# Last group's slots and four turns inside the attention's last two units, layers joined, half of the output weights split in the first expert

## The chip, the cores and the metric

The kernel runs on one core of one Trainium2 chip. Time is device microseconds of that core, from the first to the last instruction and what lies around them; the median of three runs is 391.73 us (389.76 to 392.42).

## The reference

Three layers follow one another: a retention-like attention, a soft mixture of eight experts over 32 slots, and a bilinear layer.

```python
def _attn_ref(q, k, v):                     # 8 x 8 heads, 576 positions, 64 wide
    scores = scale * np.matmul(q, k.transpose(0, 1, 3, 2))
    Dmat = np.where(rel >= 0, gamma[:, None, None] ** rel[None, :, :], 0.0)
    return np.matmul(scores * Dmat[None, :, :, :], v)

def _moe_ref(x, phi, w1, w2):               # x 4608 x 512, 8 experts of 4 slots, F = 1024
    logits = x @ phi
    d = softmax of logits over the tokens;  c = softmax of logits over the slots
    slot_input = (d.T @ x).reshape(E, S_per_e, D)
    for e in range(E):
        slot_out[e] = np.maximum(slot_input[e] @ w1[e], 0.0) @ w2[e]
    return c @ slot_out.reshape(n_slots, D)

def _moe2_ref(x, w1, w2, w3, w_out):
    return ((x @ w1) * (x @ w2) @ w3) @ w_out
```

## The kernel before, in words

All instructions are emitted in an order written out by hand (`manual_schedule`), so each engine runs its own list in program order, and SyncE (SP) issues nearly all transfers, each waiting in turn for its place.

**Attention.** 36 units `u` of 128 tokens (`NU` = 36; `T, r = divmod(u - 4, 4)` counts groups of four, which lag by four units). A unit does `emit_pv`, `emit_xt` (VectorE writes the unit's x into `xts[u % 6]`), `emit_state`, `emit_qk` of unit u + 2, `emit_turns` (L210: eight transposes of x of unit u - 4 into the PSUM tile `pair`, and one ScalarE copy to `xgs`), and `emit_inter`. Every fourth unit does the running softmax of a group: `emit_logits`, `emit_exp`, `emit_dT` (transpose of the weights, copied by ScalarE to `dt`), `emit_z` and `emit_slots` (eight matmuls into a slot sum, which VectorE adds to `acc`). Behind the loop the tail (L835 to L902) does what is left for the last two groups: `emit_logits(8)`, `emit_slots(7)`, four transposed x (`emit_xtr`), the column maxima, `emit_slots(8)` and the scaling that gives `slotm`, the input of the experts.

**Pieces.** The weights `wo`, `m1`, `m2` and `w3` come as 64-bit words in 40 pieces of 512 KB. `conv_list` (L489) turns a piece into float32 by two ScalarE and three VectorE operations, and `add` (L520) ends it on GpSimd. Pieces of `m1`, `m2` stay in `mw_sb`; pieces of `wo` (j < 8) and `w3` pass through three slots of `vals` and are split into a high and a low part, by a ScalarE cast (`copy`, L528) and a GpSimd subtraction (`sub`, L533). `emit_Ws` (L552) emits steps of the product w3 x wo, three matmuls each, 64 in all; step 4 i + k reads piece i of w3 and quarter 4 (i % 2) + k of `wo`.

**Experts.** Weights come in 64 loads of 512 KB (`load_expert`, L578), eight to an expert, each into a place from the list `free`; 21 places of 4 KB a partition are used for the attention's buffers first and come free near its end. For expert e, `emit_l1` (32 matmuls), ScalarE's relu to `hr`, VectorE's transpose to `ht` (`emit_turned`, at tick 1), and `emit_l2` (16 matmuls) at tick 2 of four. In each tick steps of `emit_Ws` are emitted up to a target written in L956, and `soft` emits the softmax over the slots, whose odd steps put two transposes on TensorE. After the experts come `a`, `b` and their products (L993 to L1105) and nine output groups (L1117).

Of the kernel before, what the change touches and what calls it, by code (L numbers as in the profile page):

```python
# [31 lines left out]
def retention_softmoe_bilinear(  # L32
# [51 lines left out]
    wop = const.tile([128, 8192], F32R, name="wop")  # L84
# [45 lines left out]
    ring = [place("ew0")]  # L130

# [76 lines left out]
    turned = pair.rearrange("p (a z k j) -> p z a k j", a=2, z=2, k=4)  # L208

# [251 lines left out]
    woh, wol = wop[:, 0:4096], wop[:, 4096:8192]  # L461
# [8 lines left out]
    nth = lambda j: j if j < 8 else j - 16  # L470

    def value(j):
        t = mw_sb[:, 512 * (j - 8):] if 8 <= j < N3 else vals[:, 512 * (nth(j) % 3):]
        return t[:, 0:512]
# [39 lines left out]
    def high_low(j):  # L514
        if j < 8:
            return woh[:, 512 * j:512 * j + 512], wol[:, 512 * j:512 * j + 512]
        t = block(w3p, (j - N3) % 3)
        return t[:, 0:512], t[:, 512:1024]

    def add(i):  # L520
# [3 lines left out]
        if not 8 <= j < N3:  # L524
            copies.append(j)
# [26 lines left out]
    def emit_Ws(n, lag=1):  # L552
        for _ in range(n):
            i, k = divmod(nW[0], 4)
            if i == 16 or nsplit[0] < min(9 + i + lag, 24):
                return
# [5 lines left out]
            bh, bl = (t[:, 512 * k8:512 * k8 + 512] for t in (woh, wol))  # L562
# [92 lines left out]
    with tc.manual_schedule():  # L655
# [72 lines left out]
        free.extend(ring)  # L728
        came, TWICE, PACED = [], (10, 14, 18, 22, 26), 3

        def can_conv():
# [3 lines left out]
            return 8 <= j < N3 or nth(j) < nsplit[0] + 3  # L735
# [14 lines left out]
        for u in range(NU):  # L750
# [51 lines left out]
            if u >= 2:  # L802
                ended = emit_turns(u - 4, u + 4)
# [16 lines left out]
            if u >= 7 and r == 3:  # L820
# [20 lines left out]
        free.extend([*p_places, s_place])  # L841
# [8 lines left out]
        emit_slots(T - 1, False)  # L850
        emit_exp(T)
        add_slots(T - 1)
        emit_z(T - 1)
        emit_z(T)
        mfin = st["m"]
        pr = bank[0]
        emit_xtr(NU - 4)
# [5 lines left out]
        emit_xtr(NU - 3, nc.vector.tensor_copy)  # L863
        emit_dT(T)
        emit_xtr(NU - 2)
        emit_xtr(NU - 1, nc.vector.tensor_copy)
        free.extend(xt_places)
# [54 lines left out]

        nsoft = [0]
# [14 lines left out]
        for e in range(NE):  # L938
# [11 lines left out]
            for t in range(4):  # L950
# [5 lines left out]
                emit_Ws(max(0, (min(5, 3 + step), min(7, 1 + step), min(55, 7 + (step - 8) * 48 // 20))[min(e, 2)] - nW[0]))  # L956
                if e == NE - 1 and t == 1:
                    emit_Ws(3, 0)
                if t == 2:
                    emit_l2(e)  # L960
                    if len(wplaces) < 8:
# [20 lines left out]
        left = [t for t in map(tag_of, qb + vb + rb + kb + p_places + [s_place, kt_place] + xt_places) if t not in [second, *map(tag_of, wplaces)]]  # L982
# [7 lines left out]
        ph, pl = (wop[:, 4096 * i:4096 * i + 4096].rearrange("p (c n) -> p c n", c=8) for i in range(2))  # L990
# [224 lines left out]
```

## Time and profile before

| what | us |
|---|---|
| median of three runs | 391.73 (389.76 to 392.42) |
| the profiled execution, whole | 393.84 |
| its span, first to last instruction | 392.1 |
| TensorE busy | 375.4 (96%) |
| VectorE, ScalarE, GpSimd busy | 257.4, 199.0, 172.6 |
| attention, to the last `emit_pv` | 0 to 161 |
| tail, to the first expert's layer 1 | 161 to 172.7 |
| experts, to the end of the last layer 2 | 172.7 to 246.3 |
| products | 246 to 281 |
| output groups | 281 to 392 |

The stages are read from the first matmul of their lines in the trace. A matmul's end in it is modelled, so busy TensorE time can hold waits; where an engine really stood is told by the wait in brackets behind a row.

### The profile page before, as it was taken

The numbers are of one execution on the slowest core, as the hardware profiler recorded it, in microseconds if no ns is written. First come the engines' busy times: TensorE is split into PE (matmuls) and PEld (weight loads), VectorE is DVE, ScalarE is ACT, GpSimd is POOL, SyncE is SP. The second block draws the span as 40 slices with busy tenths as digits, with TensorE's granted clock in tenths as the row PEclk, the third lists the DMA queues.
The fourth block names the chain that finished last, engine by engine and source line by source line (L and its number), as shares of the span: only waits on it lengthen the run. The fifth ranks groups of instructions, "written<-read, shape, count | busy, mean of one in ns | idle before, by whom it ended". The sixth has DMA issues, their size and how long they took to land.

```text
span 392.1 us, 10958 instructions
## 1 busy us (share of the span) xinstructions
PE 375.4 (96%) x4447; PEld 284.9 (73%) x4447; DVE 257.4 (66%) x432; ACT 199.0 (51%) x424; POOL 172.6 (44%) x158
## 2 busy tenths in 40 slices
PE   6999999999997999799999999999999999999996
PEld 3888787878876897564666664678688777788774
DVE  4648999899896889555477963399766445355500
ACT  2347696788675787423364532234445353544432
POOL 2733765675464436202345652127544334552420
PEclk9999999999999999999999999999999999999999
DMA  7999899899988999999999999692359989998634
GB/s 241 335 331 333 301 365 323 252 375 376 291 274 313 305 324 331 325 397 371 410 409 408 410 407 389 153 210 39 82 114 207 232 221 227 235 222 210 158 89 103
DMA packets 48211, 108.75 MB, mean 277 GB/s; under 512 B 7584, under 2 KB 10016, under 8 KB 48160
## 3 DMA queue, kind: packets, MB, share of 16 engines
q1 hardware_dynamic: 47008, 107.85, 86.4%
q8 instruction: 35, 0.57, 0.6%
q10 hardware_dynamic: 1152, 0.20, 0.3%
q14 instruction: 16, 0.13, 0.1%
HBM read 97.41 MB, written 10.62 MB: 275 GB/s over the span
## 4 chain that ended last, share of the span: by engine, by line
PE 74%; DVE 14%; DMA 8%; issue 2%; ACT 1%; POOL 1%; ACTq 0%; POOLq 0%; DVEq 0%
PE bank L564 10%; PE bank L1131 9%; PE bank L1133 8%; PE bank L1132 8%; PE output L282 6%; PE scores L253 5%; DMA kr<-in_v 4%; PE output L316 4%; PE bank L622 3%; PE bank L602 3%; PE state L296 3%; DMA v<-in_ew 2%; PE one L356 2%; PE bank L1122 2%; PE pair L215 2%; DVE vals L497 2%
## 5 line engine op out<-in xcount | busy, mean ns | idle before, releaser
L646 POOL TENSOR_TENSOR cc<-mw_sb,cc 128x512 fp32r<-128x512 f32 x36 | 46.0, 1297 | 56.5 <-ACT cc L645 56.5
L523 POOL TENSOR_TENSOR vals<-vals,msb 128x512 int32<-128x512 int32 x24 | 30.8, 1284 | 46.7 <-DVE vals L497 44.5
L564 PE MATMUL bank<-wop,w3p 128*128 128x512 f32 x192 | 50.0, 404 | 0.0
L263 DVE TENSOR_TENSOR pm<-scores,msb 128x1024 f32<-128x1024 f32 x31 | 37.8, 1220 | 15.0 <-PE scores L253 14.8
L564 PEld LDWEIGHTS bank<-wop,w3p 128*128 128x128 f32 x192 | 34.4, 188 | 14.4 <-issue 7.1
L645 ACT CAST cc<-mw_sb 128x512 fp32r<-128x512 f32 x36 | 22.2, 616 | 43.6 <-DVE mw_sb L644 34.8
L1131 PE MATMUL bank<-w3p,cc 128*128 128x512 f32 x108 | 43.1, 399 | 0.0
L1133 PE MATMUL bank<-w3p,cc 128*128 128x512 f32 x108 | 42.1, 390 | 0.0
L1132 PE MATMUL bank<-w3p,cc 128*128 128x512 f32 x108 | 42.0, 389 | 0.0
L253 PE MATMUL scores<-q,kt 64*128 64x128 f32 x496 | 36.6, 285 | 2.0 <-issue 2.0
L644 DVE TENSOR_TENSOR mw_sb<-lga,raw 128x512 f32<-128x512 f32 x32 | 29.3, 955 | 12.3 <-POOL cc L646 12.1
L282 PE MATMUL output<-pm,v 128*64 128x128 f32 x512 | 36.1, 284 | 1.0 <-issue 1.0
L523 POOL TENSOR_TENSOR mw_sb<-mw_sb,msb 128x512 int32<-128x512 int32 x16 | 20.4, 1276 | 33.9 <-DVE mw_sb L497 25.7
L1135 ACT ACTIVATE mw_sb<-bank,rz 128x512 f32<-128x512 f32 x36 | 24.7, 685 | 19.0 <-PE bank L1133 9.4
L253 PEld LDWEIGHTS scores<-q,kt 64*128 64x128 f32 x496 | 30.3, 187 | 4.8 <-issue 2.9
L533 POOL TENSOR_TENSOR w3p<-vals,w3p 128x512 fp32r<-128x512 f32 x16 | 21.2, 1326 | 28.7 <-ACT w3p L528 19.8
L282 PEld LDWEIGHTS output<-pm,v 128*64 128x64 f32 x512 | 28.1, 139 | 6.1 <-issue 4.9
L220 ACT COPY kt<-pair 128x512 f32<-128x512 f32 x26 | 15.2, 585 | 29.1 <-PE pair L219 29.1
L504 ACT ACTIVATE msb<-raw 128x512 int32<-128x512 uint32 x40 | 27.8, 696 | 0.0
L192 POOL TENSOR_TENSOR k<-kr,msb 128x512 f32<-128x512 f32 (+1 forms) x30 | 25.9, 886 | 3.9 <-DMA kr<-in_v 3.9
L1131 PEld LDWEIGHTS bank<-w3p,cc 128*128 128x128 f32 x108 | 20.3, 188 | 7.1 <-issue 2.9
L503 DVE TENSOR_SCALAR vals<-vals 128x512 f32<-128x512 f32 x24 | 18.5, 772 | 7.6 <-ACT vals L502 7.6
(226 smaller groups left out, 775.3 us busy)
## 6 DMA issues: line engine op xcount, KB each, us to landing
q<-in_q SPq DMA_DIRECT2D x20, 512.0 KB, 6.5
raw<-expt SPq DMA_DIRECT2D x36, 256.0 KB, 4.4
kr<-in_v SPq DMA_DIRECT2D x16, 512.0 KB, 6.0
v<-in_v SPq DMA_DIRECT2D x16, 512.0 KB, 6.8
raw<-in_m SPq DMA_DIRECT2D x16, 512.0 KB, 6.2
raw<-in_w SPq DMA_DIRECT2D x16, 512.0 KB, 6.1
out_x<-mw_sb SPq DMA_DIRECT2D x64, 128.0 KB, 2.4
q<-in_ew SPq DMA_DIRECT2D x14, 512.0 KB, 10.1
```

Of the source, the lines that this page charges most:

```text
L192: (nc.vector if first else nc.gpsimd).tensor_tensor(out=Ks[:, :, 0:m, h], in0=K[:, 1 - h, :, 0:m], in1=ktab(c, h)[:, 0:m].unsqueeze(1).uns ...
L253: last = nc.tensor.matmul(out=ps[:, p], lhsT=ktb[u % 2][a, p], rhs=Q[a, :, x, p], start=True, stop=True)
L263: nc.vector.tensor_tensor(out=p_places[u % 2].rearrange("p (g t) -> p g t", g=8), in0=(pair if u == 1 else scores).rearrange("p (g t) -> p ...
L282: last = nc.tensor.matmul(out=xt_view(p)[side(p, h)], lhsT=v_tile(u)[:, 1 - h, x, p], rhs=p_main(u)[:, h, p], start=(block_of(u) == 0 and ...
L504: lambda: nc.scalar.activation(out=p.bitcast(I32), in_=lo, func=ACTF.Copy, scale=2.0 ** -29),
L523: nc.gpsimd.tensor_tensor(out=ti, in0=ti, in1=parts[i % 2].bitcast(I32), op=ALU.add)
L564: nc.tensor.matmul(out=ps, lhsT=x, rhs=y, start=(k8 == 0 and part == 0), stop=(k8 == 7 and part == 2))
L644: eng.tensor_tensor(out=e, in0=x, in1=y[:, m], op=ALU.mult)
L646: nc.gpsimd.tensor_tensor(out=cl[m], in0=e, in1=ch[m], op=ALU.subtract)
L1131: nc.tensor.matmul(out=ob, lhsT=ch[m][:, sl], rhs=gh[m], start=False, stop=False)
L1132: nc.tensor.matmul(out=ob, lhsT=ch[m][:, sl], rhs=gl[m], start=False, stop=False)
L1133: nc.tensor.matmul(out=ob, lhsT=cl[m][:, sl], rhs=gh[m], start=False, stop=(m == 3))
```

## The change

- At unit 34 the turns of x of units 30 and 31 are done together (`emit_two_turns`), and `emit_dT(7)` follows them; at unit 35 `emit_slots(7)`, `emit_z(7)` and the turns of x 32 and 33. The tail keeps two `emit_xtr`, whose copies are held until the maxima are done, and has a fourth step of `emit_Ws`.
- `wop` shrinks from 8192 to 4096 columns. Only quarters 0 to 3 of `wo` are split in the attention; 4 to 7 are converted into two new places (`wv0`, `wv1`) and split behind the first expert's layer 2 (`split_late`: four ScalarE casts, four GpSimd subtractions) into four places taken from `free`.
- Two more places (`ew1`, `ew2`) take expert weights during the attention.
- Layer 2 of each expert moves from tick 2 to tick 3, next to layer 1 of the following expert. The targets of `emit_Ws` change: none in expert 0, one in expert 1, then 55 by the end of expert 6 as before.

```diff
@@ -81,7 +81,7 @@
     block = lambda t, i, n=1: t[:, 1024 * i:1024 * (i + n)]
 
     mw_sb = const.tile([128, 8192], F32, name="mw_sb")
-    wop = const.tile([128, 8192], F32R, name="wop")
+    wop = const.tile([128, 4096], F32R, name="wop")
     w3p = const.tile([128, 3072], F32R, name="w3p")
 
     NRAW = 4
@@ -128,6 +128,8 @@
     rb = [place(f"kr{i}") for i in range(RBUF)]
     kb = [place(f"k{i}") for i in range(KBUF)]
     ring = [place("ew0")]
+    spare = [place("ew1"), place("ew2")]
+    wv_places = [place("wv0"), place("wv1")]
 
 
     lo, hi = slice(0, 64), slice(64, 128)
@@ -206,6 +208,15 @@
         copy(out=ktb[u % 2].rearrange("p k t -> p (k t)"), in_=ps)
 
     turned = pair.rearrange("p (a z k j) -> p z a k j", a=2, z=2, k=4)
+
+    def emit_two_turns(xu):
+        for z in range(2):
+            for p in range(4):
+                for h, a in halves:
+                    last = nc.tensor.transpose(turned[:, z, h, p], xts[(xu + z) % 6][a, p], ident[a, a])
+        for z in range(2):
+            nc.scalar.copy(out=xgs[(xu + z) % 4].rearrange("p (k a j) -> p a k j", k=4, a=2), in_=turned[:, z])
+        return last
 
     def emit_turns(xu, ku):
         last = None
@@ -458,7 +469,10 @@
 
 
     pieces = []
-    woh, wol = wop[:, 0:4096], wop[:, 4096:8192]
+    NWO = 4
+    nth = lambda j: j if j < 8 else j - 24 + NWO
+    wv = both(wv_places[0]) + both(wv_places[1])
+    wo_parts = [(wop[:, 1024 * i:1024 * i + 512], wop[:, 1024 * i + 512:1024 * i + 1024]) for i in range(NWO)]
     for i in range(8):
         pieces.append(wo[:, 512 * i:512 * i + 512])
     for i in range(16):
@@ -467,9 +481,9 @@
         pieces.append(w3[i // 2][:, 512 * (i % 2):512 * (i % 2) + 512])
     N3 = 24
     turn = [j for i in range(8) for j in (i, 8 + i)] + list(range(16, len(pieces)))
-    nth = lambda j: j if j < 8 else j - 16
-
     def value(j):
+        if NWO <= j < 8:
+            return wv[j - NWO]
         t = mw_sb[:, 512 * (j - 8):] if 8 <= j < N3 else vals[:, 512 * (nth(j) % 3):]
         return t[:, 0:512]
 
@@ -513,7 +527,7 @@
 
     def high_low(j):
         if j < 8:
-            return woh[:, 512 * j:512 * j + 512], wol[:, 512 * j:512 * j + 512]
+            return wo_parts[j]
         t = block(w3p, (j - N3) % 3)
         return t[:, 0:512], t[:, 512:1024]
 
@@ -521,7 +535,7 @@
         j = turn[i]
         ti = value(j).bitcast(I32)
         nc.gpsimd.tensor_tensor(out=ti, in0=ti, in1=parts[i % 2].bitcast(I32), op=ALU.add)
-        if not 8 <= j < N3:
+        if not NWO <= j < N3:
             copies.append(j)
 
     def copy(j):
@@ -552,14 +566,14 @@
     def emit_Ws(n, lag=1):
         for _ in range(n):
             i, k = divmod(nW[0], 4)
-            if i == 16 or nsplit[0] < min(9 + i + lag, 24):
+            if i == 16 or nsplit[0] < min(NWO + 1 + i + lag, NWO + 16):
                 return
             nW[0] += 1
             ps = bank[(5, 2)[i // 2 % 2]]
             b = block(w3p, i % 3)
             ah, al = (b[:, o + 128 * k:o + 128 * k + 128] for o in (0, 512))
             k8 = 4 * (i % 2) + k
-            bh, bl = (t[:, 512 * k8:512 * k8 + 512] for t in (woh, wol))
+            bh, bl = wo_parts[k8]
             for part, (x, y) in enumerate(((ah, bh), (ah, bl), (al, bh))):
                 nc.tensor.matmul(out=ps, lhsT=x, rhs=y, start=(k8 == 0 and part == 0), stop=(k8 == 7 and part == 2))
             if k8 == 7:
@@ -725,14 +739,14 @@
         output_factors(0)
         output_factors(1)
 
-        free.extend(ring)
+        free.extend([*ring, *spare])
         came, TWICE, PACED = [], (10, 14, 18, 22, 26), 3
 
         def can_conv():
             if nconv[0] == nl[0]:
                 return False
             j = turn[nconv[0]]
-            return 8 <= j < N3 or nth(j) < nsplit[0] + 3
+            return NWO <= j < N3 or nth(j) < nsplit[0] + 3
 
         def next_conv(u):
             if not conv_ops and nconv[0] < len(came) and came[nconv[0]] <= u and can_conv():
@@ -799,7 +813,14 @@
             if u >= 8 and r == 0:
                 emit_z(T - 1)
                 emit_slots(T - 1)
-            if u >= 2:
+            if u == NU - 2:
+                ended = emit_two_turns(u - 4)
+                emit_dT(T)
+            elif u == NU - 1:
+                emit_slots(T)
+                emit_z(T)
+                ended = emit_two_turns(u - 3)
+            elif u >= 2:
                 ended = emit_turns(u - 4, u + 4)
             if u + 1 < NU:
                 ended = emit_inter(u + 1) or ended
@@ -817,7 +838,7 @@
                     later(lambda k=k: load_q(k + QBUF))
                 else:
                     free.append(qb[k % QBUF])
-            if u >= 7 and r == 3:
+            if 7 <= u < NU - 1 and r == 3:
                 emit_dT(T)
             run_conv(1)
             if u != 1:
@@ -838,7 +859,7 @@
         run(subs)
         run_copies()
         run(adds)
-        free.extend([*p_places, s_place])
+        free.extend([*p_places, s_place, xt_places[0]])
         load_expert(4)
         load_pieces()
         close_pool("psum")
@@ -847,24 +868,23 @@
         misc[:] = [bank[6], bank[7], bank[2], bank[4]]
         nc.gpsimd.memset(slotm, 0.0)
         emit_logits(T)
-        emit_slots(T - 1, False)
+        held = []
+        hold = lambda engine: lambda **kw: held.append(lambda: engine(**kw))
+        emit_xtr(NU - 2, hold(nc.scalar.copy))
         emit_exp(T)
-        add_slots(T - 1)
-        emit_z(T - 1)
-        emit_z(T)
+        emit_xtr(NU - 1, hold(nc.vector.tensor_copy))
         mfin = st["m"]
         pr = bank[0]
-        emit_xtr(NU - 4)
         nc.tensor.matmul(out=pr[0:1, 0:128], lhsT=mfin, rhs=ident, start=True, stop=True)
         mrow = tmp.tile([1, 32, 1], F32, tag="h0", name="mrow")
         nc.vector.tensor_reduce(out=mrow, in_=pr[0:1, 0:128].rearrange("p (g s) -> p s g", g=4), axis=AX.X, op=ALU.max)
         nrow = tmp.tile([1, 4, 32], F32, tag="h1", name="nrow")
         nc.vector.tensor_scalar(out=nrow, in0=mrow.rearrange("p s x -> p x s").to_broadcast([1, 4, 32]), scalar1=-1.0, scalar2=None, op0=ALU.mult)
-        emit_xtr(NU - 3, nc.vector.tensor_copy)
+        run(held)
+        emit_Ws(1, 0)
         emit_dT(T)
-        emit_xtr(NU - 2)
-        emit_xtr(NU - 1, nc.vector.tensor_copy)
-        free.extend(xt_places)
+        emit_z(T)
+        free.extend(xt_places[1:])
         load_expert(7)
         nc.tensor.matmul(out=bank[1][:, 0:1], lhsT=nrow.rearrange("p g s -> p (g s)"), rhs=ident[0:1, 0:1], start=True, stop=True)
         negm = tmp.tile([128, 1], F32, tag="negm", name="negm")
@@ -920,6 +940,16 @@
             run(evicts)
 
 
+        def split_late():
+            homes = [free.pop(0) for _ in range(8 - NWO)]
+            for j, t in enumerate(homes, NWO):
+                t = place(tag_of(t), f"wo{j}", F32R)
+                wo_parts.append((t[:, 0:512], t[:, 512:1024]))
+                nc.scalar.copy(out=wo_parts[j][0], in_=value(j))
+                nc.gpsimd.tensor_tensor(out=wo_parts[j][1], in0=value(j), in1=wo_parts[j][0], op=ALU.subtract)
+            free.extend(wv_places)
+            return homes
+
         nsoft = [0]
 
         def soft():
@@ -953,11 +983,13 @@
                     emit_turned(e)
                 load_expert(8)
                 step = 4 * e + t + 1
-                emit_Ws(max(0, (min(5, 3 + step), min(7, 1 + step), min(55, 7 + (step - 8) * 48 // 20))[min(e, 2)] - nW[0]))
+                emit_Ws(max(0, (4, min(5, step - 3), min(55, 5 + (step - 8) * 50 // 20))[min(e, 2)] - nW[0]))
                 if e == NE - 1 and t == 1:
                     emit_Ws(3, 0)
-                if t == 2:
+                if t == 3:
                     emit_l2(e)
+                    if e == 0:
+                        homes = split_late()
                     if len(wplaces) < 8:
                         wplaces.append(free.pop(0))
                     load_expert(8)
...
@@ -1041,11 +1073,11 @@
                 v.tensor_tensor(out=t2[:, c - 1:b - 1], in0=base(ab[1], cb, b - c), in1=win(af, cb, c, b - c), op=ALU.mult)
                 v.tensor_tensor(out=t1[:, a:b], in0=base(af, cb, b - a), in1=win(ab[1], cb, a, b - a), op=ALU.mult)
                 v.tensor_tensor(out=t1[:, c:b], in0=t1[:, c:b], in1=t2[:, c - 1:b - 1], op=ALU.add)
-                nc.scalar.copy(out=ph[:, cb, 32 * a:32 * b], in_=t1[:, a:b].rearrange("p a b -> p (a b)"))
+                nc.scalar.copy(out=ph[cb][:, 32 * a:32 * b], in_=t1[:, a:b].rearrange("p a b -> p (a b)"))
 
         def pairs_low(cb):
             t1 = sums(cb).rearrange("p a b -> p (a b)")
-            nc.vector.tensor_tensor(out=pl[:, cb, 0:512], in0=t1, in1=ph[:, cb, 0:512], op=ALU.subtract)
+            nc.vector.tensor_tensor(out=pl[cb], in0=t1, in1=ph[cb], op=ALU.subtract)
 
         GB = (0, 1, 5, 3)
 
...
```

The hunks left out change only which places and views the later stages use.

## Rows read from the trace of the kernel before

**Rows 1.** The page: busy share of the DMA engines in 40 slices, in tenths.
```profile
DMA  7999899899988999999999999692359989998634
```

**Rows 2.** Chain that ended last, 182 to 245 us: start, length, what.
```profile
182.27 1.85 PE bank L622 x16
...
235.85 9.50 DMA v<-in_ew
```

**Rows 3.** Timeline of SP, last issues: start, length, line, transfer.
```profile
232.60 0.33 SPq L583 DMA_DIRECT2D k<-in_ew  x1
233.88 0.33 SPq L583 DMA_DIRECT2D q<-in_ew  x1
```

**Rows 4.** Timeline of PE in the expert stage; in brackets idle before, and releaser.
```profile
196.59 5.07 PE L564 MATMUL bank<-wop,w3p 128*128 128x512 f32 x21
...
202.48 0.60 PE L622 MATMUL bank<-xts,ht 128*32 128x512 f32 x2
...
202.91 0.60 PE L622 MATMUL bank<-xts,ht 128*32 128x512 f32 x2
203.44 0.33 PE L409 MATMUL bank<-cst,et 128*128 128x128 f32 x1
...
245.39 1.05 PE L622 MATMUL bank<-v,ht 128*32 128x512 f32 x4 [0.26 <-DMA v<-in_ew]
```

**Rows 5.** Timeline of PE and ACT from the end of attention to the first expert.
```profile
159.97 0.69 PE L316 MATMUL output<-q,st 64*64 64x64 f32 x32 [1.04 <-DVE xts L327]
...
161.06 0.47 PE L215 MATMUL pair<-cst,xts 64*128 64x64 f32 x8
161.57 0.58 ACT L222 COPY xg<-pair 128x512 f32<-128x512 f32 x1 [1.94 <-PE pair L215]
162.37 1.08 PE L356 MATMUL bank<-xts,cst 128*32 128x128 f32 x32 [0.59 <-ACT dt L431]
163.91 1.07 PE L445 MATMUL bank<-xg,dt 128*32 128x512 f32 x8 [0.46 <-issue]
166.40 1.04 PE L346 MATMUL bank<-cst,xts 128*128 128x128 f32 x8
172.72 0.64 PE L602 MATMUL bank<-ew,slotm 128*32 128x256 f32 x8
```

**Rows 6.** Timeline of expert 0's relu, exponential and transpose, and expert 2's first layer.
```profile
174.72 0.38 ACT L607 ACTIVATE hr<-bank 128x256 f32<-128x256 f32 x1 [6.08 <-PE bank L602]
175.00 0.30 ACT L398 ACTIVATE et<-et 128x128 f32<-128x128 f32 x1
175.13 0.45 DVE L615 STREAM_TRANSPOSE ht<-hr 128x256 f32<-128x256 f32 x1 [0.99 <-ACT hr L607]
...
183.94 1.48 PE L602 MATMUL bank<-xts,slotm 128*32 128x256 f32 x24
```

**Rows 7.** Groups by line: count, busy us, mean ns, idle before and releaser.
```profile
L502 ACT ACTIVATE vals<-raw 128x512 f32<-128x512 f32 x24 | 16.5, 687 | 3.1 <-DMA raw<-in_w 3.0
L503 DVE TENSOR_SCALAR vals<-vals 128x512 f32<-128x512 f32 x24 | 18.5, 772 | 7.6 <-ACT vals L502 7.6
L505 DVE TENSOR_SCALAR vals<-vals 128x512 uint32<-128x512 uint32 x24 | 14.9, 622 | 0.7
L533 POOL TENSOR_TENSOR wop<-vals,wop 128x512 fp32r<-128x512 f32 x8 | 10.8, 1348 | 0.0
```

**Rows 8.** Windows: stretch, length, busy time (PE first), granted clock, DMA share, GB/s.
```profile
120.00:124.00 4.00, 3.59 (x113) 1.00 0.75 230
124.00:128.00 4.00, 2.40 (x28) 0.71 0.97 363
128.00:132.00 4.00, 4.00 (x73) 0.86 0.77 201
...
160.00:165.00 5.00, 3.95 (x114) 2.52 (x115) 1.36 (x5) 1.37 (x6) 1.67 (x2) 1.00 0.91 300
```

**Rows 9.** Timeline of PE at the longest stall of the attention.
```profile
125.60 0.32 PE L253 MATMUL scores<-q,kt 64*128 64x128 f32 x1 [2.01 <-issue]
```

More of the change, by code (lines that the diff above doesn't have):

```diff
@@ L981, in retention_softmoe_bilinear @@
         two = lambda tag, n: [t[:, o:o + 512] for t in [place(tag, n, F32R)] for o in (0, 512)]
-        left = [t for t in map(tag_of, qb + vb + rb + kb + p_places + [s_place, kt_place] + xt_places) if t not in [second, *map(tag_of, wplaces)]]
+        left = [t for t in map(tag_of, qb + vb + rb + kb + p_places + [s_place, kt_place] + xt_places + spare + wv_places) if t not in [second, *map(tag_of, homes), *map(tag_of, wplaces)]]
         cs2 = two(left[0], "cs")
@@ L989, in retention_softmoe_bilinear @@
         y16 = [vals[:, 512 * i:512 * i + 512] for i in range(2)]
-        ph, pl = (wop[:, 4096 * i:4096 * i + 4096].rearrange("p (c n) -> p c n", c=8) for i in range(2))
+        ph, pl = zip(*wo_parts)
         ab = [t.rearrange("p (c s) -> p c s", c=8) for t in (mw_sb[:, 3584:4096], parts[0])]
@@ L1056, in g_mm @@
                 nc.tensor.matmul(
-                    out=bank[GB[m]], lhsT=a[:, cb, sl], rhs=b[cb],
+                    out=bank[GB[m]], lhsT=a[cb][:, sl], rhs=b[cb],
                     start=(cb == 0 and i == 0), stop=(cb == 7 and i == 2), skip_group_check=True,
```

## The prediction

> **What bounds the kernel now.** I read the slices of the page first, then the chain that ended last, then the timelines of the tail and of the experts. In slices 17 to 25 the DMA engines are full [rows 1]: from the attention's end until the last expert load has landed, transfers never pause. SP's last loads go out 1.28 us apart [rows 3], the pace at which 512 KB drain. The chain [rows 2] crosses that stage on TensorE and leaves it only once, for the last load: issued at 235.85, landed at 245.35. But TensorE is no freer than the transfers: the load's matmuls waited for 0.26 us only [rows 4], and between 184 and 245 one group of matmuls starts where the one before ends. So two bounds meet at 245.4: the transfers, and TensorE's work plus the gaps it had before 184. A gain needs both to move. Gaps of TensorE stand at the seam: 1.04 us ahead of `emit_inter(35)`, 0.59 ahead of the last logits, 0.46 ahead of `emit_slots(7)` [rows 5].
>
> **The tail.** The last `emit_pv` gives way at 161.06 and the first expert starts at 172.72 [rows 5]: 11.66 us, with three W steps (one is three of the 21 matmuls in 5.07 us, 0.72 us [rows 4]).
> - Unit 34's extra turn and `emit_dT(7)` fall into the 1.04 us wait, which goes on waiting for VectorE: they cost nothing there. Without that cover they would cost about 0.8 (0.47, and 0.33, the length of a lone 128-column transpose [rows 4, 5]).
> - At 161.06 come `emit_slots(7)`, 1.07 less the overlap, so 1.0, and from 162.1 two turns. A copy starts 0.51 after its turn did (161.06 to 161.57) and takes 0.58 [rows 5]; two end at 163.75. The last logits' bank is half of `pair`, which both copies read, so they can't start sooner: 163.8 instead of 162.37. TensorE stands 0.8 us there, from the turns' end at about 162.9. The bounds of this wait: nothing if only the first copy is awaited or the bank comes free by columns, 1.1 if the second copy starts only when the first has wholly ended.
> - From the logits to layer 1 were 10.35 us (162.37 to 172.72). Out go the 0.46 wait, `emit_slots(7)` (1.07) and two of four transposed x (1.04 [rows 5]); in comes a W step, 0.72: 8.5. Layer 1 of expert 0 starts at 172.3, 0.4 earlier, with one W step more done. The held copies lie beside this W step.
>
> **Experts 0 and 1.** Call that start S. Layer 1 ends at S + 1.9 or so (it was followed by the relu at S + 2.0 and VectorE's transpose at S + 2.4 [rows 6]). Before, W steps lay over this; now expert 0 has none. And VectorE's list now has the conversion of piece 30 ahead of the transpose, since `sub` of piece 27 has moved into tick 0: relu to S + 2.4, exponential to S + 2.6 [rows 6], abs 0.69, clamp 0.77, shift 0.62 [rows 7], transpose 0.45: `ht` at S + 5.1. TensorE has only two transposes of `soft` meanwhile, about 0.4. Layer 2 runs from S + 5.1, layer 1 of expert 1 behind it, each 1.8 (1.85 [rows 2]), to S + 8.7. There ScalarE's relu and exponential (0.7), two transposes and one W step (1.1) cover `ht`; layer 2 from S + 10.5, expert 2 from S + 12.3, at 184.6. It was 183.94 [rows 6]: 0.6 later. Bounds: 2.1 less if the conversion doesn't hold `ht` (it would be there at S + 2.9, and layer 2 start behind the transposes at S + 3.0); 1.3 more if the abs must wait for a GpSimd subtraction's whole 1.35, that of piece 27, to give its slot of `vals` free.
> By then 5 W steps are done where 7 were: 2 x 0.72 = 1.4 us more work for the dense stretch. The four casts (0.58 each, as the copies of [rows 5]) start as layer 2 gives their places free, the first at S + 5.6, and lie on ScalarE beside TensorE's layers; the four subtractions (1.35 each, 5.4 in all [rows 7]) follow piece 30's add on GpSimd, from about S + 7.1 to S + 12.5. W step 4, at S + 9.8, needs the first alone, steps 5 to 7 the rest from S + 14.1 on (behind expert 2's layer 1); without that cover the price is one subtraction, 1.35.
>
> **Layers joined.** Where layer 2 met another operation there was a gap of 0.10: its pairs of matmuls start 0.43 apart (202.48, 202.91), and the next operation at 203.44 instead of 203.34 [rows 4]. Five experts save it: 0.5. Nothing else of that move is paid: layer 2 frees its places a tick (some 2 us) later, but eight loads in the queue are 10 us of transfers.
>
> **Transfers.** Counted back from 245.35 at 1.28: 45 loads (19 to 63) and 6 pieces, 65.3 us, so loads up to 18 had landed by 180.0. With `ew1` and `ew2` the same places of the program issue two loads more, at units 19 and 23. The engines had room: shares of 0.75 and 0.77 in two windows behind unit 23 [rows 8], 1.9 us in these two alone against 2.6 to be moved. So loads up to 20 are there by 180.0. Loads 21, 22 and a piece follow by 183.9. Load 23 goes into `wv1`, which the last two subtractions read, and SP is in order: it can't go before S + 12.5 = 184.8, and loads 24 to 30, though their places are free, queue behind it. The engines run dry for 1 to 3 us (a lone load's landing isn't shown: between its 1.28 and the 9.50 of a queued one; I take 2 with the wait). From 185.9 on 41 loads and 5 pieces, 58.9 us, end at 244.8, half a microsecond before; between 242.8 (no pause) and 246.5. What hides the two loads, if that cover is gone: 2.6 us of transfers ahead of attention's own.
>
> **The attention's engines.** Four casts and four subtractions leave units 14 to 21 (2.3 us of ScalarE, 5.4 of GpSimd [rows 5, 7]). TensorE is the fullest there, so I take nothing; the bound is one subtraction's 1.35, were a unit held by it.
>
> **Sum.** Expert 2 0.6 later, W steps 1.4, joined -0.5, and the wait of 0.26 for the last load is gone: +1.2 us on TensorE, and its 246.6 or so lies behind the transfers' 244.8 plus the last pairs (1.0). Behind it nothing changes but names of places. The profiled execution took 393.84 with its span of 392.1, 2.1 above the median of 391.73; I add the sum to both: 395.0 profiled, **392.9** median.
>
> **The clock.** At 125.60 TensorE had stood 2.01 us for nothing that shows [rows 9]; the granted clock was 0.71 and 0.86 in the two windows from 124 to 132 [rows 8], so 3.4 us at 1.2 GHz (2 x (0.29 + 0.14) x 4), 1.7 us of work lost. Behind the wait of 1.04 [rows 5] the clock was 1.00 [rows 8]. The new gap in expert 0 is 3.2 with 0.4 of transposes in it, nearer to the 2.01 in its longer part (S + 3.2 to 5.1).
> The Trainium skill, "TensorE: Matmul & The Clock Gate", Part 1, says that the slow clock is the default and that only activity lifts it; by that rule the gap would be punished and the sum be +2.9, by the row of 1.04 it stays +1.2. The windows from 124 to 132 [rows 8] agree with the rule in kind.
>
> **Rivals.**
> 1. The clock falls in expert 0's gap: +1.2 + 1.7 = 394.6. For it the 1.9 us part, against it the transposes between. 0.25.
> 2. Faster: the 2.01 us stall at 123.6 and its 1.7 of clock go, since from unit 23 to 27 SP's order is shifted by a load. Nothing shows as its cause [rows 9]. It decides from whether that stall is there at all: 391.73 + 1.2 - 3.7 = 389.2. 0.15.
> 3. The change doesn't do what it says: the two loads aren't hidden and delay the attention by up to 2.6: 395.5. Against it the shares of 0.75. 0.08.
> 4. The gap is shorter, as the conversion doesn't hold `ht`: transfers then set the end, -0.5: 391.2. Against it VectorE's fixed order. 0.12.
>
> **How the numbers follow.** The forecast, 392.9, has 0.40 (its own range 392.0 to 393.8, by the wait at the logits and the subtractions). The range from 389.2 to 395.1 leaves out rival 3 and the far sides, 2 in 10 with what I haven't thought of. One per cent, 3.9 us, is about what a measurement tells from no change. Below 387.8 needs rival 2 with a second gain: 0.06; above 395.6 needs rivals 1 and 3 together: 0.10; within, 0.84.
>
> **What would show it.** Right: the last logits 0.8 us behind the turns with ScalarE's copy as releaser; layer 1 of expert 0 near 172 with four W steps ahead of it; `ht` of expert 0 behind the shift on VectorE and a gap of 3 us on TensorE; SP holding a load for GpSimd near 185; no wait for the last load. Wrong: layer 2 of expert 0 within 1.5 us of its layer 1, a wait of more than 1 us for the last load, a different length of attention, or a stage behind 246 that isn't as long as before.

## The result, and the profile after

The changed kernel took 394.60 us, the median of 9 runs (392.50 to 396.85), beside 391.73 for the kernel before (9 runs, 389.76 to 392.48): a ratio of 1.0065, interval 1.0037 to 1.0093. Run again beside other runs of the kernel before it stood at 393.83 to 392.14, 1.0033 (1.0005 to 1.0060). So it is slower by 0.3 to 0.7 per cent: within one per cent, inside the range, on the side that was forecast, and 1.7 us above the forecast of 392.9. Its profiled execution took 394.85 with a span of 393.1; before it was 393.84 and 392.1.

The page of the changed kernel first: the granted clock and the DMA share in slices, as in [rows 1].

```profile
span 393.1 us, 10987 instructions
...
PEclk9999999999999999998999999999999999999999
DMA  7999899899979999997999999692259989999644
```

The slices hardly differ from those of before, and the stages lie where they lay. The chain that ended last (start, length, what) answers [rows 2] and [rows 9]: the stall of "issue" in the attention is there again, and the chain leaves TensorE for a load of an expert's weights, now at expert 6's layer 1.

```profile
123.70 1.65 issue
...
176.10 2.80 PE bank L636 x16
...
220.86 10.17 DMA v<-in_ew
```

TensorE from the attention's end to expert 2, and at the late waits (start, length, line, operands; in brackets the idle time before and its releaser), answers [rows 4, 5, 6]. L327 is `emit_inter(35)`, L367 the last logits, L616 layer 1 and L636 layer 2 of an expert, L578 a W step, L420 and L401 the transposes of `soft`:

```profile
159.66 0.69 PE L327 MATMUL output<-q,st 64*64 64x64 f32 x32 [0.53 <-DVE xts L338]
...
162.76 1.29 PE L367 MATMUL bank<-xts,cst 128*32 128x128 f32 x32 [0.30 <-DVE acc L467]
...
171.64 1.50 PE L616 MATMUL bank<-ew,slotm 128*32 128x256 f32 x24
...
174.27 0.33 PE L420 MATMUL bank<-cst,et 128*128 128x128 f32 x1 [0.70 <-ACT et L409]
174.44 0.27 PE L401 MATMUL bank<-cst,lga 128*128 128x128 f32 x1
176.10 0.62 PE L636 MATMUL bank<-k,ht 128*32 128x512 f32 x2 [1.39 <-DVE ht L629]
...
177.80 1.07 PE L636 MATMUL bank<-k,ht 128*32 128x512 f32 x2
...
178.66 1.10 PE L616 MATMUL bank<-kt,slotm 128*32 128x256 f32 x8
...
185.00 0.61 PE L616 MATMUL bank<-pm,slotm 128*32 128x256 f32 x8
...
231.07 0.64 PE L616 MATMUL bank<-v,slotm 128*32 128x256 f32 x8 [0.57 <-DMA v<-in_ew]
...
246.41 0.62 PE L636 MATMUL bank<-k,ht 128*32 128x512 f32 x2
```

A pair of layer 2's matmuls at 176.1 takes 0.62, one at 177.80 takes 1.07: in between the granted clock fell to its lower level, 1.2 GHz. The windows (length; busy time of PE, PEld, DVE, ACT, POOL with counts; granted clock; DMA share; GB/s) show that, and the hole in the transfers behind it:

```profile
178.00:180.00 2.00, 2.00 (x24) 0.71 (x18) 1.71 (x5) 1.43 (x3) 2.00 (x3) 0.50 1.05 414
180.00:182.00 2.00, 1.44 (x24) 0.57 (x16) 0.03 (x1) 0.49 (x3) 2.00 (x3) 0.90 0.61 238
182.00:184.00 2.00, 1.81 (x13) 0.95 (x17) 1.80 (x7) 0.41 (x2) 0.97 (x1) 1.00 0.10 23
184.00:186.00 2.00, 2.00 (x32) 0.91 (x28) 0.79 (x4) 0.31 (x1) 0.00 (x0) 1.00 0.78 248
186.00:188.00 2.00, 2.00 (x25) 1.24 (x14) 0.45 (x1) 0.39 (x1) 0.00 (x0) 1.00 0.94 311
```

SP's issues answer [rows 3]. Nothing was issued from 176.68 to 183.00, then the load into `wv1` and the queue behind it; the last load went out at 240.01 and landed at 246.37, where before it was 235.85 and 245.35 [rows 2]:

```profile
176.68 0.33 SPq L493 DMA_DIRECT2D raw<-in_w  x1
183.00 0.33 SPq L597 DMA_DIRECT2D wv<-in_ew  x1
...
240.01 0.33 SPq L597 DMA_DIRECT2D k<-in_ew  x1
```

What SP waited for are GpSimd's late subtractions, which read `wv0` and `wv1`. They end at 182.97, one after the other behind the add of piece 30:

```profile
176.76 1.27 POOL L537 TENSOR_TENSOR vals<-vals,msb 128x512 int32<-128x512 int32 x1 [3.34 <-DVE vals L511]
177.99 4.98 POOL L949 TENSOR_TENSOR wo<-wv,wo 128x512 fp32r<-128x512 f32 x4
```

The stages read off these timelines, in us. E is where the last `emit_pv` gives way to the next operation, S the start of expert 0's layer 1, X2 that of expert 2's, "end" the end of the last layer 2; "again" is the second profile of the changed kernel. What comes behind "end" lasts 145.6 to 145.7 in every profile of this study, so the difference lies ahead of it. E itself spreads from 158.75 to 162.43 over the 14 profiles, and from 158.75 to 162.06 over the 12 of the changed kernel and the edits to it, so the stages are compared from E on.

| | E to S | S to X2 | X2 to end | E to end | span |
|---|---|---|---|---|---|
| before | 11.66 | 11.22 | 62.50 | 85.38 | 392.1 |
| after (clock fell) | 10.89 | 13.36 | 62.46 | 86.71 | 393.1 |
| after, again (it didn't) | 10.67 | 11.68 | 64.49 | 86.84 | 393.4 |

The two profiles of one kernel are the first clue. One lost 1.7 us in expert 0, the other didn't, and they end alike: the second gave the time back later. There three operations of expert 6's layer 1 wait for loads (the second profile, TensorE's timeline):

```profile
228.72 0.64 PE L616 MATMUL bank<-wv,slotm 128*32 128x256 f32 x8 [0.90 <-DMA wv<-in_ew]
229.99 0.64 PE L616 MATMUL bank<-kt,slotm 128*32 128x256 f32 x8 [0.64 <-DMA kt<-in_ew]
231.26 0.64 PE L616 MATMUL bank<-v,slotm 128*32 128x256 f32 x8 [0.63 <-DMA v<-in_ew]
```

They start 1.27 apart, the pace of the loads. It looks as if the transfers set the end and not TensorE; the experiments test that.

### The profile page after: what moved, and what is told of

It reads as the page before. It is cut to its first block, busy times and chain, and to the rows that moved or that the text cites. A ratio compares the mean times of both kernels' runs of the same rounds, so it can differ in the third digit from the quotient of the medians.

```text
span 393.1 us, 10987 instructions
## 1 busy us (share of the span) xinstructions
PE 374.8 (95%) x4455; PEld 285.4 (73%) x4455; DVE 253.4 (64%) x431; ACT 200.4 (51%) x425; POOL 171.8 (44%) x158
## 4 chain that ended last, share of the span: by engine, by line
PE 71%; DMA 9%; DVE 8%; POOL 4%; SPq 3%; issue 3%; ACT 1%; POOLq 0%; DVEq 0%; ACTq 0%
PE bank L1163 9%; PE bank L578 8%; PE bank L1165 8%; PE bank L1164 8%; PE output L293 6%; PE scores L264 6%; DMA kr<-in_v 4%; PE output L327 4%; PE bank L616 3%; PE bank L636 3%; PE state L307 3%; DMA v<-in_ew 3%; SPq L430 2%; PE one L367 2%; PE one L456 2%
## 5 line engine op out<-in xcount | busy, mean ns | idle before, releaser
L537 POOL TENSOR_TENSOR vals<-vals,msb 128x512 int32<-128x512 int32 x20 | 25.8, 1290 | 41.1 <-DVE vals L511 36.6
L658 DVE TENSOR_TENSOR mw_sb<-lga,raw 128x512 f32<-128x512 f32 x32 | 29.3, 954 | 12.3 <-POOL cc L660 12.1
L578 PE MATMUL bank<-wop,w3p 128*128 128x512 f32 x96 | 25.4, 402 | 0.0
L1163 PEld LDWEIGHTS bank<-w3p,cc 128*128 128x128 f32 x108 | 20.2, 188 | 7.0 <-issue 2.9
L578 PE MATMUL bank<-wo,w3p 128*128 128x512 f32 x96 | 25.3, 401 | 0.0
L1165 PEld LDWEIGHTS bank<-w3p,cc 128*128 128x128 f32 x108 | 20.3, 188 | 4.4
```

What stands on the lines that cost most here:

```text
L537: nc.gpsimd.tensor_tensor(out=ti, in0=ti, in1=parts[i % 2].bitcast(I32), op=ALU.add)
L578: nc.tensor.matmul(out=ps, lhsT=x, rhs=y, start=(k8 == 0 and part == 0), stop=(k8 == 7 and part == 2))
L658: eng.tensor_tensor(out=e, in0=x, in1=y[:, m], op=ALU.mult)
L1163: nc.tensor.matmul(out=ob, lhsT=ch[m][:, sl], rhs=gh[m], start=False, stop=False)
L1165: nc.tensor.matmul(out=ob, lhsT=cl[m][:, sl], rhs=gh[m], start=False, stop=(m == 3))
```

## The experiments

The theory of the first six: the transfers set the end, and the pause near 182 makes them late. Against it: the gap of TensorE in expert 0 and the clock that falls behind it (rival 1), the two prefetch loads (rival 3), and the order of the layers. Edits are to the changed kernel unless something else is said; medians stand beside the kernel before in the same set of runs.

**The changed kernel again (e0).** No edit.

> The changed kernel as it is, beside the next three on one chip. All theories: 1.004 to 1.009 of the kernel before, and in its profile the gap of TensorE ahead of expert 0's layer 2, the fall of the clock behind it, and a pause of the transfers of about 3 us near 182 us until GpSimd's last subtraction frees the place of load 23.

Measured: 393.83 to 392.14, ratio 1.0033 (1.0005 to 1.0060), and the second profile above. The difference is there again, smaller; the clock stayed up in expert 0 and nothing was won.

**The places of the late values freed later (e1).** `wv0` still joins the list of free places there, `wv1` only behind expert 1's layer 1, so that loads with other places come first.

```diff
 def split_late():
-    free.extend(wv_places)
+    free.append(wv_places[0])
 # expert loop, behind last = emit_l1(e)
+    if e == 1:
+        free.append(wv_places[1])
```

> The second of the two places that the late split frees is handed out only behind expert 1's layer 1, so load 23 takes a place of that layer and no load waits for the late subtractions. Theory of the dry queue: loads 23 to 26 go out near 179 to 181 instead of 183, the pause of the transfers shrinks from 3.3 us to 1 or less, the last load lands about 2 us earlier, near 244, and the whole is 1 us below the changed kernel, less if TensorE's own delay (gap and clock) then sets the end. Theory of the clock: the last load is earlier but the end of the last layer 2 moves by less than 0.7 us, since TensorE arrives late at expert 2.

Measured: 390.92 to 392.14, ratio 0.9984 (0.9952 to 1.0015). This one edit takes back what the change lost, 2.9 us below e0 where 1 was expected; how much of that is the clock's is taken up with the rivals below. SP issues the loads ahead of the one into `wv1`:

```profile
178.78 0.33 SPq L493 DMA_DIRECT2D raw<-in_w  x1
182.31 0.33 SPq L597 DMA_DIRECT2D kt<-in_ew  x1
...
185.49 0.33 SPq L597 DMA_DIRECT2D wv<-in_ew  x1
```

Its profiled execution is slower than its median (span 394.1): the clock fell twice in it, near 25 and in expert 0, and TensorE stands 0.79 inside the last logits for nothing that shows. The pause is smaller there, not gone: 2.47 lie between the landing of the last piece ahead of it and that of the next load, 3.86 in the changed kernel. X2 to end is 61.30, 1.2 shorter than before, without waits for loads.

**The gap of expert 0 filled (e3).** Six matmuls whose result nobody reads stand ahead of expert 0's layer 2; this work is added.

```diff
 if t == 3:
+    for _ in range(6 if e == 0 else 0):
+        nc.tensor.matmul(out=bank[1], lhsT=wo_parts[0][0][:, 0:128],
+                         rhs=wo_parts[1][0], start=True, stop=True)
     emit_l2(e)
```

> Six matmuls whose result nobody reads (128x512, 1.4 us in all) are added in the gap of TensorE ahead of expert 0's layer 2, which goes on waiting for its transposed input. Theory of the clock: the clock stays at 2.4 GHz there, expert 0's layer 2 and expert 1's layer 1 take 1.85 and 1.8 us instead of 2.8 and 2.7, expert 2 starts 1 to 1.7 us earlier, near 183.7, and the whole is 0.5 to 1.5 us below the changed kernel. Theory of the dry queue: load 23 goes out about 0.7 us earlier at most, since the casts begin with layer 2's ends, and the whole changes by less than 0.7 us.

Measured: 393.81, ratio 1.0041 (1.0009 to 1.0073): nothing gained, as the theory of the transfers expected. The clock held in the profile, and S to X2 is 11.68, but X2 to end is 64.21, with the same three waits at expert 6 (0.63, 0.61, 0.63, from 226.74). In the windows (as above) the clock is 1.00 and the hole in the transfers is still there:

```profile
174.00:178.00 4.00, 3.92 (x50) 1.46 (x48) 3.86 (x8) 2.18 (x4) 3.07 (x3) 1.00 1.03 410
178.00:182.00 4.00, 3.33 (x33) 1.55 (x37) 3.14 (x8) 1.03 (x4) 3.18 (x3) 1.00 0.22 83
```

**Expert 0's transpose ahead of the conversion (e4).** VectorE makes `ht` first.

```diff
-if t == 1:
+if t == 1 and e:
     emit_turned(e)
 # between soft() and the conversion
+if e == 0 and t == 0:
+    emit_turned(e)
```

> Expert 0's transpose on VectorE is emitted ahead of the conversion of piece 30 instead of behind it. Both theories: the transpose runs 1.2 us earlier, layer 2 starts 3.0 us behind the start of layer 1 instead of 4.5, near 174.7. Theory of the clock: the gap is then too short for a fall, expert 2 starts 2.5 to 3 us earlier, and the whole is 1 to 2.5 us below the changed kernel. Theory of the dry queue: the late split starts 1.4 us earlier, load 23 goes out 1.4 us or more earlier, near 181.3, and the whole is 1 to 1.5 us below; the clock makes no difference of its own.

Measured: 393.95, ratio 1.0046 (1.0017 to 1.0076). Both theories had expected 1 us or more, and neither got it. The gap all but went (layer 2 at S + 3.0, S to X2 11.25), but the load into `wv1` went out only 0.2 earlier, at S + 11.2, as GpSimd's subtractions still came behind its add of piece 30, and TensorE ran into the loads all the same:

```profile
227.32 0.64 PE L616 MATMUL bank<-wv,slotm 128*32 128x256 f32 x8 [0.61 <-DMA wv<-in_ew]
228.59 0.64 PE L616 MATMUL bank<-kt,slotm 128*32 128x256 f32 x8 [0.63 <-DMA kt<-in_ew]
229.85 0.64 PE L616 MATMUL bank<-v,slotm 128*32 128x256 f32 x8 [0.62 <-DMA v<-in_ew]
```

From E to end the profiles of e3 and e4 take 86.58 and 86.11, the two of the changed kernel 86.71 and 86.84: in these profiles TensorE's gap and the clock behind it make 0.1 to 0.7 us of the loss as long as the transfers are late.

**Layer 2 back in tick 2 (e2).**

```diff
-if t == 3:
+if t == 2:
     emit_l2(e)
```

> Layer 2 of every expert back at tick 2, all else as in the changed kernel. Theory of the dry queue: load 23 goes out at the same time (layer 2 of expert 0 waits for its transposed input either way), the pause stays 3 us, the joined layers' 0.5 us is lost on TensorE but the places of each layer 2 come free 2 us earlier; the whole within 0.7 us of the changed kernel. Theory of the late layer 2 (the move to tick 3 itself costs the time, by freeing places late): 1.5 to 2.5 us below the changed kernel.

Measured: 393.82 to 392.40, ratio 1.0054 (1.0023 to 1.0086), the changed kernel's own. The joint gains nothing that shows here; what it is worth comes with e9. Its profile waits for no load at expert 6, though its loads come no earlier: the clock fell in expert 0's gap, S to X2 is 14.14, and TensorE itself was as late as they (E to end 87.30).

**The tail's part alone (e5).** The kernel before with only the hunks of units 34 and 35 and of the tail.

```diff
+            if u == NU - 2:
+                ended = emit_two_turns(u - 4)
+                emit_dT(T)
+            elif u == NU - 1:
+                emit_slots(T)
...
-        emit_xtr(NU - 2)
-        emit_xtr(NU - 1, nc.vector.tensor_copy)
```

> The kernel before with the attention's and the tail's part of the change alone: two turns each in units 34 and 35, slots and the fourth W step moved, one place freed earlier. The layer 1 of expert 0 starts 1.0 us earlier, near 171.7, and TensorE has one W step more behind it. As the transfers set the end of the expert stage in the kernel before too (its last load lands at 245.35), the theory of the dry queue expects 0 to 0.7 us below the kernel before. The rival, that TensorE's path sets the end, expects 1.0 to 1.8 us below.

Measured: 392.20, ratio 1.0021 (0.9986 to 1.0056): no difference that can be told, and not the 1.0 to 1.8 that TensorE's path as the bound would have given. The profile shows why nothing comes of it by itself: E to S stays at 11.71 (one W step more lies in it, and the logits stand 0.82 for nothing that shows), and S to X2 is 12.08, 0.9 longer, since with that W step gone from expert 0 its layer 2 stands 1.63 for `ht`. But X2 to end is 61.35, 1.15 shorter than before, and E to end 85.14. What TensorE lost ahead of X2 it had back at the end, where it no longer waited for the last load: in the kernel before it was TensorE that had slack, and the transfers set the end.

**Without the two prefetch places (e6).** They join `free` in the tail, as in a kernel that doesn't prefetch with them.

```diff
-        free.extend([*ring, *spare])
+        free.extend(ring)
...
-        free.extend([*p_places, s_place, xt_places[0]])
+        free.extend([*spare, *p_places, s_place, xt_places[0]])
```

> The two more places are handed out at the tail instead of the attention's start, so the two loads of units 19 and 23 go out behind unit 35. Theory of the dry queue: the loads ahead of the pause fill it, load 23 still waits for the late split, the last load lands at the same time, the whole within 0.5 us of the changed kernel: the prefetch is worth nothing there. If the prefetch is worth its transfers: 2.6 us slower than the changed kernel. If its loads disturb the attention: the attention ends up to 1 us earlier.

Measured: 393.42, ratio 1.0048 (1.0013 to 1.0082), as with them. The loads that are missing ahead of the pause are transferred in it: the DMA share from 178 to 186 is 0.81, with the prefetch 0.63 (one window of 8 us of each profile). The two loads were hidden in the attention, as the change meant, and were then given away to an idle stretch.

**Both mends (e7, and again e11).** The edits of e1 and e4 together. The theory now: two bounds, and a version that moves both beats the kernel before.

> Both mends: the second place of the late split handed out behind expert 1's layer 1, and expert 0's transpose ahead of the conversion. Theory of the dry queue: the pause is gone and TensorE is not late, so what the transpose gains now counts: 1 us or more below the kernel with the first mend alone, 1.5 to 2.5 below the kernel before, no wait for a transfer of more than 0.5 us on TensorE until the last layer 2. If TensorE's path was the bound all along, the second mend alone would have shown it, and the two together give no more than the first.

> The kernel with both mends again, beside the next three on one chip: 0.993 to 0.997 of the kernel before; the transfers of the experts end some 3 us ahead of the last layer 2, so TensorE's path sets the end there now.

Measured: 390.05 to 392.40, ratio 0.9950 (0.9918 to 0.9982), and on another chip 390.50 to 393.21, 0.9944 (0.9914 to 0.9974). Faster than both kernels, twice, by half a per cent of the kernel before. The profile of e11 has a span of 388.0 and no hole from 178 to 182:

```profile
178.00:182.00 4.00, 3.83 (x41) 1.86 (x45) 3.34 (x8) 0.70 (x3) 2.88 (x3) 1.00 1.02 410
```

TensorE waits for no load there. e4's edit is worth nothing without e1's. Beside it, it shortens S to X2 from 11.68 to 11.26; the intervals of e1 and e7 overlap, so the times don't show that gain by themselves.

**Both mends, and the softmax of the selections later (e8).** As e7, with no `soft` step in expert 0's last three ticks and expert 1's first three, and one for each tick from there on.

```diff
-while e < NE - 1 and nsoft[0] <= (4 * e + t) * 18 // 28:
+while e < NE - 1 and nsoft[0] <= (4 * e + t) * 18 // 28 and 4 * e + t not in range(1, 7):
     soft()
+    if e:
+        break
```

> Both mends, and the softmax over the slots emits nothing from tick 1 of expert 0 to tick 2 of expert 1 and then one step a tick until it has caught up. In the kernel with both mends TensorE stood 1.8 us in expert 1 behind a transpose of that softmax, which waited for small VectorE operations stretched to 1.2 us each beside GpSimd's subtractions. If TensorE's path sets the end: expert 2 starts 1.0 to 1.8 us earlier behind the start of expert 0, and the whole is 0.7 to 1.8 us below the kernel with both mends. If the transfers still set it: no change.

Measured: 390.72 to 393.21, ratio 0.9929 (0.9896 to 0.9962). S to X2 is 10.39, 0.9 shorter (1.0 to 1.8 had been expected), and X2 to end 0.5 longer (61.82 to 61.30), presumably since the steps come later. The median cannot be told from e11's; the 0.7 to 1.8 that had been expected of it did not come.

**Both mends, layer 2 in tick 2 (e9).** As e7, with e2's edit.

> Both mends, and layer 2 back at tick 2: what joining the layers is worth where TensorE's path sets the end. By the gap of 0.10 us that each joint saves: 0.5 us slower than the kernel with both mends, hardly to be told apart from nothing. If the later layer 2 costs by its late places: faster by 0.5 us or more.

Measured: 391.64 to 393.21, ratio 0.9989 (0.9963 to 1.0016), 1.1 us behind e11. X2 to end is 62.49, with the joint 61.30: the joint is worth 1.2 us where the transfers don't set the end, and the 0.5 that was expected missed by more than half.

**Both mends, no prefetch (e10).** As e7, with e6's edit.

> Both mends, and the two loads of units 19 and 23 handed out at the tail: the transfers of the experts end up to 2.6 us later, which lies within the some 3 us by which they lead. If TensorE's path sets the end, within 0.7 us of the kernel with both mends; if the transfers do, 1.5 to 2.6 us slower.

Measured: 392.68 to 393.21, ratio 1.0002 (0.9965 to 1.0039), 2.2 us behind e11. Of the two cases expected, 0.7 at most and 1.5 to 2.6, it is the second, for transfers that set the end. Their lead had been put at 3 us; in e11 the last load landed at 240.23, 2.0 ahead of the end. In e10 the transfers run full from 178 to 188 and are still late at expert 6 (TensorE's timeline):

```profile
230.54 0.64 PE L616 MATMUL bank<-v,slotm 128*32 128x256 f32 x8 [0.59 <-DMA v<-in_ew]
```

So the prefetch is worth some 2 us once the pause is gone (2.2 by the medians, 1.8 from E to end), near the 2.6 that two loads drain in, and nothing as long as it is there (e6).

## Why the prediction held, and where its working failed

**The step that failed is the one that chose the bound.** The prediction had TensorE set the end near 247.6, with the transfers done at 244.8 and hidden. In fact the last load landed at 246.4 and TensorE waited for loads. The sum of +1.2 lies close to the +1.3 to +1.5 of E to end (86.71 and 86.84 to 85.38) by luck, because two errors cancelled: TensorE's side was 2.9 too long, and the transfers' side 1.6 too short.

**TensorE's side, term by term.**
- Logits: forecast at 163.8 behind two ScalarE copies; they started at 162.76 behind VectorE's `acc`, after 0.30. The copies did not hold them: this is the lower bound of that wait, which had been named. From there to S it took 8.88 (8.5 forecast); S came at 171.64 (172.3).
- `ht` was held by VectorE's conversion, as forecast, but less: clamp and shift took 0.43 each, not the 0.77 and 0.62 of [rows 7], which are means over the whole kernel. Layer 2 started at S + 4.46 (5.1), and X2 at S + 11.68 without the clock's fall (12.3). VectorE's timeline of the changed kernel shows the order that was forecast, the two steps of the conversion ahead of the transpose:

```profile
174.80 0.43 DVE L517 TENSOR_SCALAR vals<-vals 128x512 f32<-128x512 f32 x1 [1.74 <-ACT vals L516]
175.26 0.43 DVE L519 TENSOR_SCALAR vals<-vals 128x512 uint32<-128x512 uint32 x1
175.61 0.44 DVE L629 STREAM_TRANSPOSE ht<-hr 128x256 f32<-128x256 f32 x1
```

- The joint is worth 1.2 (e9), not 0.5. Only the 0.10 behind layer 2 had been counted, not the gap that goes ahead of layer 1: in the chains a layer 1 takes 1.86 behind W steps (before) and 1.73 behind layer 2 (after), 0.13 at each of the five joints.

```profile
227.71 1.86 PE bank L602 x32
```
```profile
207.42 1.73 PE bank L616 x32
```

- The wait for the last load in the kernel before was not 0.26 but about 1.3. [rows 4] gave a matmul's row, whose end is modelled. The track of the weight loads of the kernel before, which was not read, shows longer ones (idle time in brackets, not all of it a wait):

```profile
244.08 0.14 PEld L622 LDWEIGHTS bank<-q,ht 128*32 128x32 f32 x4 [0.74 <-DMA q<-in_ew]
...
245.39 0.14 PEld L622 LDWEIGHTS bank<-v,ht 128*32 128x32 f32 x4 [1.17 <-DMA v<-in_ew]
```

  The whole of that layer 2 took 3.26, where one without a wait takes 1.93: 1.3 us. The prediction drew from the 0.26 that both bounds met; in truth the transfers came 1.3 us after TensorE was ready, the slack that e5 shows too.
- With the W steps' 1.4, which no run contradicts, X2 to end becomes 62.50 + 1.4 - 1.2 - 1.3 = 61.4; e1, e7 and e11, which don't wait for loads, have 61.30 to 61.31. So TensorE alone would have taken E to end to 10.67 + 11.68 + 61.3 = 83.65, 1.7 less than before, where the prediction had 1.2 more. e11, with 0.43 less in S to X2, has 83.22.

**The transfers' side.** The mechanism was right: SP held a load for GpSimd's last subtraction on `wv1`, until 183.00 (184.8 forecast), with the rest of the queue behind it. The size was not. The landings of the loads say where the 1.6 lies. The last piece ahead of the pause landed at 183.12 and the load into `wv1` at 186.98, 3.86 later where 1.28 is the pace: 2.6 lost, not 2. Since the engines had drained 0.8 earlier than forecast, that landing was still 0.2 earlier than in the sum (185.9 and 1.28). But the 45 transfers behind it took 59.4 us, not 57.6. The next two landed 1.76 and 1.52 apart, 0.7 lost: the queue came back slowly, at 248 and 311 GB/s in the two windows from 184 to 188, where 410 is full. Another 1.1 was lost in one interval, from 195.39 to 197.80, for which nothing here shows the cause (e7 to e9 lose 0.7 near the same place, e11 nothing). The last load landed 1.30 behind the one before it, at the pace. A queue that has run dry was nowhere in the sum, which had 1.28 for every load behind the pause.

**The rivals.** Rival 1's event came as described: the clock fell at about 177.0, behind the gap of 0.70 and 1.39, and S to X2 is 1.7 longer for it (13.36 to 11.68), the price that it had. But its time, 394.6, which is the median of the first set, does not follow from it in the two profiles: with and without the fall E to end is the same to 0.13. The Trainium skill, "TensorE: Matmul & The Clock Gate", Part 1, has the slow clock as the default that only activity lifts; the trace agrees on the fall (granted clock 0.50 from 178 to 180), and what it cost in these two executions was decided by the transfers. Rival 2 was wrong: the stall is there (123.70, 1.65). Of rival 3 nothing shows: the attention ended at 160.75, before at 161.06, and the 2.6 us are not there. Rival 4 named the right bound, the transfers, for the wrong reason and with an end 1.6 too early.

**What stays open of rival 1.** The mean granted clock was below 0.9975 (in the profiles, at least one fall of 3.4 us) in 16 of 21 executions of the changed kernel and in 21 of 98 of the kernel before, and in either kernel those take about 2 us longer on average. That alone makes some 1.1 of the 1.4 us between the two averages (393.8 and 392.4). At equal clock the changed kernel is 0.2 slower without a fall (392.2 in 5 executions, 392.0 in 77) and 0.5 with one (394.3 in 16, 393.8 in 21). In expert 0 the clock fell in four of the five profiles of versions that have the whole gap (the first of the changed kernel, e1, e2, e6; not e0), and in none of the nine others. So the greater part of the slowdown may be the clock's, and rival 1 is not refuted.

For the transfers speak the waits and stages of the profiles, and the other versions at the full clock: the four that hand out `wv1` as the changed kernel does (e2, e3, e4, e6) average 393.0 in 19 executions, the kernel before beside them 391.8 in 52, e1 390.5 in 7. e1's gain over e0 is 1.6 at the full clock (from 392.1) and 1.3 with a fall (394.1 to 392.8), of the 2.9 between their medians. And filling the gap (e3) left 7 of 11 executions at the full clock and the median where it was. What share of the changed kernel's own loss is the transfers' and what the clock's, these runs don't settle.

**The signs that had been listed.** Right: four W steps ahead of S near 172, `ht` behind VectorE's shift, SP held by GpSimd (183.0 for "near 185"), nearly no wait for the last load. Smaller than listed: the gap of TensorE, 2.5 from layer 1's end to layer 2 with 0.4 of transposes in it. Missing: ScalarE's copy as the releaser of the logits. In e1, e5, e7, e9 and e10 the logits stand 0.24 to 0.82 more, for nothing that shows. None of the signs of "wrong" came, and yet the step was wrong: the wait for a load stood at expert 6's layer 1, which the list had not got.

## What to carry to other kernels

Where two bounds meet at the end of a stage, a change that relieves one gains nothing, and one that relieves one and delays the other loses; size both to the same accuracy before choosing which of them decides, and then mend both (e1 alone at 0.998, e4 alone at 1.005, together at 0.995). In an in-order DMA queue the place that is freed last must not be the first that is handed out: here four subtractions on an engine that is busy for 44% of the span stopped loads whose places were free, and another order of a list of places won 1.3 to 1.6 us at equal clock (e1). Read a wait for a load on the track of the weight loads too, not from the bracket of a matmul alone.

## What the runs showed of the hardware that was not expected

Operations of VectorE on four columns became six to seven times as long beside GpSimd's subtractions. The timeline of VectorE with both mends (e7), of the same two lines within 8 us:

```profile
177.78 1.23 DVE L415 TENSOR_SCALAR zz<-zz 128x4 f32<-128x4 f32 x1
...
179.25 0.97 DVE L418 TENSOR_TENSOR rz<-rz 128x4 f32<-128x4 f32 x1
...
185.20 0.17 DVE L415 TENSOR_SCALAR zz<-zz 128x4 f32<-128x4 f32 x1
...
185.62 0.16 DVE L418 TENSOR_TENSOR rz<-rz 128x4 f32<-128x4 f32 x1
```

GpSimd's rows of that profile say where they end: its add ends at 178.98 and the first of the four subtractions, 1.27 long, at 180.20, and the two long operations end at 179.00 and 180.22.

```profile
177.69 1.29 POOL L537 TENSOR_TENSOR vals<-vals,msb 128x512 int32<-128x512 int32 x1 [3.14 <-DMA xts<-in_ew]
178.93 4.97 POOL L949 TENSOR_TENSOR wo<-wv,wo 128x512 fp32r<-128x512 f32 x4
```

The Trainium skill, "SBUF — State Buffer", section "Who interferes with whom", says that VectorE and GpSimd share a pair of ports; that VectorE needs it for operations with two inputs in SBUF and in its two-port modes, which `tensor_scalar` can enter; and that whoever comes first has it for the whole instruction while the other blocks fully. The trace agrees: one is a `tensor_scalar`, the other a `tensor_tensor` on two inputs in SBUF, and each ends within 0.03 us of GpSimd's instruction. That it lengthens the path of `soft` (in e7 TensorE stands 1.79 us ahead of a transpose of `soft` at 181.20) was not tried by itself; e8 moves those steps away from the subtractions, and its S to X2 is 0.9 shorter.
